# Cutting the run of small products in a fused attention and MLP kernel, and planning with other durations

## The chip, the cores and the metric

The kernel runs on one core of a Trainium2 chip. Time is device microseconds of one execution, and lower is better. Five engines work side by side: TensorE (PE in the profile, with its weight loads as PEld), VectorE (DVE), ScalarE (ACT), GpSimd (POOL) and SyncE (SP), which here issues most of the transfers. Each engine takes its instructions in the order in which the program gives them, and waits where an operand is not there yet.

## The reference

Two stages. The first is a linear attention with a state for each of 4 batches and 8 heads, over 768 time steps of 48 channels; the second is an MLP with a piecewise gate over the 3072 tokens that result.

```
for t in range(S):
    cur = einsum('bhd,bhe->bhde', u[None] * kt, vt)
    y[:, :, t] = einsum('bhd,bhde->bhe', rt, state + cur)
    state = wt[:, :, :, None] * state + einsum('bhd,bhe->bhde', kt, vt)
x = y as (3072, 384)
h = x @ w_in                     # 384 x 2048
g = where(h >= 1, h, where(h <= -1, 0, (h + 1)**2 / 4))
return g @ w_out                 # 2048 x 384
```

All inputs and the result are float32, and the kernel keeps that precision: in the MLP a float32 operand is split into a high and a low part, and three products of parts stand for one.

## The kernel before

**The attention** goes through twelve units (0 to 11), each 64 time steps of all batches, 256 tokens, as one chunk: within the chunk the products of r with k are formed as small matrices, across chunks a state of 48x48 per head is carried. A unit's work on TensorE is, in order: small 64x64 products of r with k ("among", L555; VectorE then picks the causal half of them into R, L561), transposes of k (L594, copied out by ScalarE, L603), and then the *run*: 16 products of r with the old state, crosswise between heads and groups ("cross", L667), 32 products of k times v for the new state ("umat", L624), and 48 more into the same two banks as the first (16 with the old state, 32 of R with v, "along", L667). Every float32 product of these is two instructions of the profile on TensorE and two weight loads, so the run is 192 products and 192 loads in the profile's counting. From k times v VectorE forms the new state (`stepped`, L642 and the fade behind it), which the next unit's cross needs; from the two banks the unit's y is brought into x (L739, L741).

In units 1 to 10 the three parts of the run are *glued* (`plan.glue`): nothing may stand between them on TensorE. Units 0 and 11 are not glued.

**The MLP** goes through six blocks of 512 tokens (two units each) with 16 steps over the hidden width. One step is nine wide products x by w_in into a bank (`product_in`, L1272), the gate (ScalarE L1084 and L1085, VectorE L1086, ScalarE's rounding L1088, VectorE's remainder L1089), and nine wide products of the gate by w_out into three accumulators (`product_out`, L1292). The first 5 steps of block 0 and the first 14 of block 1 work on the two halves of 256 tokens apart, so that the MLP starts with one unit done. The last block uses another scheme with fewer products (L984, finished by L1036). The weights arrive packed and are unpacked on the way, during the first half of the kernel (L441 to L454).

**What sets the order.** The program declares some thousand operations to a planner (class `Plan`), each with its engine, an assumed cost in us, a due time, what it reads and what it writes. `order` simulates the engines with these costs, taking on each engine the ready operation with the earliest key; a result may be used on another engine after `HOP`. `late` goes backward through such a plan to set new keys, and `best` keeps, of 40 randomly disturbed plans with a fixed seed, the one with the smallest planned end. [...] So a changed cost can move any operation, while the duration on the chip does not follow from it.

## Time and profile before

| what | value |
| --- | --- |
| time, median of three runs | 510.96 us (509.55 to 511.69) |
| the profiled execution | 510.8 us, of which the span is 509.2 us |
| granted clock of TensorE, mean | 0.994 |
| products and weight loads on TensorE | 5583 and 5583 |
| idle time of TensorE before products of L667, ended by "issue" | 9.1 us at six places |

Times stand in us. A row of the page's groups gives line, engine, operation, written from read tiles, partitions by elements, the count; then the busy time, the mean of one in ns, and the engine's idle time just before, with what ended most of it. "issue" means that the engine waited for nothing that the profile shows: no tile, no transfer, no semaphore. Rows of a timeline give the start, the duration, the instruction, and in brackets the idle time before it. The ends of products are modelled, so that starts are compared here where tenths of a us matter.

### The profile page before, as it was taken

Reading aid. Unit: us, or ns where it says so; the run is one execution under the profiler, and the core shown is the slowest. Engines: PE = TensorE matmul, PEld = TensorE weight load, DVE = VectorE, ACT = ScalarE, POOL = GpSimd, SP = SyncE. Lnnn points to the kernel's source line nnn. Section 1 sums busy time; section 2 is a strip of 40 time slices with the busy share of each in tenths; the row PEclk is TensorE's granted clock in tenths of the full one; section 3 lists DMA queues with packets and bytes.
Section 4 is the critical chain, followed back from the end, with each engine's and each line's share of the span. In section 5 each row is a group of like instructions: output and inputs, shape, how many; then the busy total and the mean of one; then the engine's idle time right before and its main releaser. Section 6 shows DMA issues by size and latency. Waiting matters only on the chain. (4 is left out here: it accounts for less than half of the span.)

```text
span 509.2 us, 13264 instructions
## 1 busy us (share of the span) xinstructions
PE 486.8 (96%) x5583; PEld 414.9 (81%) x5583; DVE 367.0 (72%) x631; ACT 305.6 (60%) x628; POOL 97.0 (19%) x80
## 2 busy tenths in 40 slices
PE   7778999999999999998999999999999999999994
PEld 5568988888889998877888887878878878889894
DVE  6899899988798888697963377854248544596653
ACT  4577979888866656565454556454365445575550
POOL 1654414411111111123010010200002402402000
PEclk9899999999999999999999999999999999999998
DMA  8977546245633350444320132400102000010002
GB/s 302 407 277 261 209 149 235 64 126 185 203 126 137 114 173 21 147 130 154 104 84 0 63 131 84 132 1 0 63 1 59 0 1 17 19 45 1 3 0 69
DMA packets 22052, 54.72 MB, mean 107 GB/s; under 512 B 3040, under 2 KB 9184, under 8 KB 21984
## 3 DMA queue, kind: packets, MB, share of 16 engines
q1 hardware_dynamic: 21840, 53.65, 30.6%
q8 instruction: 46, 0.75, 0.6%
q14 instruction: 22, 0.18, 0.1%
q10 hardware_dynamic: 144, 0.13, 0.1%
HBM read 47.09 MB, written 4.72 MB: 102 GB/s over the span
## 5 line engine op out<-in xcount | busy, mean ns | idle before, releaser
L1272 PE MATMUL h<-x,wt 128*128 128x512 f32 (+1 forms) x1035 | 219.4, 359 | 1.8 <-DVE x L739 1.5
L1272 PEld LDWEIGHTS h<-x,wt 128*128 128x128 f32 x1035 | 170.0, 188 | 32.5 <-DVE x L739 1.7
L1292 PE MATMUL acc<-gh,wt 128*128 128x512 f32 (+1 forms) x594 | 129.5, 353 | 0.0
L1292 PEld LDWEIGHTS acc<-gh,wt 128*128 128x128 f32 x594 | 97.6, 188 | 17.0
L1086 DVE SCALAR_TENSOR_TENSOR g<-g,h 128x512 f32<-128x512 f32 (+1 forms) x99 | 57.2, 578 | 70.2 <-ACT g L1085 69.9
L1084 ACT ACTIVATE g<-h 128x512 f32<-128x512 f32 (+1 forms) x99 | 50.9, 515 | 79.0 <-PE h L1272 68.0
L1292 PE MATMUL acc<-gl,wt 128*128 128x512 f32 (+1 forms) x297 | 72.1, 351 | 0.0
L1089 DVE TENSOR_TENSOR gl<-g,gh 128x512 fp32r<-128x512 f32 (+1 forms) x99 | 62.6, 642 | 7.8 <-ACT gh L1088 6.6
L1088 ACT CAST gh<-g 128x512 fp32r<-128x512 f32 (+1 forms) x99 | 52.5, 532 | 17.6 <-DVE g L1086 10.1
L1292 PEld LDWEIGHTS acc<-gl,wt 128*128 128x128 f32 x297 | 50.3, 188 | 8.4
L1085 ACT ACTIVATE g<-g 128x512 f32<-128x512 f32 (+1 forms) x99 | 54.5, 551 | 2.9
L581 POOL TENSOR_TENSOR r<-cst,d 128x512 f32<-128x512 f32 x18 | 19.7, 1113 | 168.5 <-PE bank L667 102.6
L449 POOL TENSOR_SCALAR wraw<-fl 128x768 uint16<-128x768 f32 x13 | 40.0, 3084 | 54.6 <-ACT wraw L447 54.6
L514 DVE TENSOR_TENSOR_SCAN p<-wq,seeds 128x520 f32<-128x520 f32 x24 | 32.3, 1346 | 3.2 <-DMA wq<-in_w 2.4
L573 POOL TENSOR_TENSOR nk<-nk 128x768 f32<-128x768 f32 x9 | 17.3, 1927 | 84.1 <-DMA nk<-in_nk 84.1
L509 DVE TENSOR_TENSOR_SCAN y<-wq,seeds 128x520 f32<-128x520 f32 x24 | 30.5, 1269 | 0.8
L945 DVE SCALAR_TENSOR_TENSOR rk<-rk,h 128x512 f32<-128x512 f32 x16 | 11.0, 687 | 18.3 <-ACT rk L944 18.0
L667 PE MATMUL bank<-r,vn 64*64 64x64 f32 (+1 forms) x768 | 15.4, 223 | 9.1 <-issue 9.1
L667 PEld LDWEIGHTS bank<-r,vn 64*64 64x64 f32 (+1 forms) x768 | 13.5, 135 | 9.9 <-issue 9.9
L942 ACT ACTIVATE rk<-h 128x512 f32<-128x512 f32 x16 | 9.6, 598 | 17.9 <-PE h L1272 17.7
L741 ACT CAST x<-bank 128x384 fp32r<-128x384 f32 x24 | 11.3, 485 | 12.3 <-PE bank L667 11.3
L561 DVE COPY_PREDICATED r<-below,bank 128x512 f32<-128x512 int32 x23 | 16.1, 734 | 3.3 <-PE bank L555 3.3
(198 smaller groups left out, 614.3 us busy)
## 6 DMA issues: line engine op xcount, KB each, us to landing
rk<-in_rk SPq DMA_DIRECT2D x24, 512.0 KB, 4.4
wraw<-in_wbits SPq DMA_DIRECT2D x16, 768.0 KB, 7.1
nk<-in_nk SPq DMA_DIRECT2D x9, 768.0 KB, 4.6
wq<-in_w SPq DMA_DIRECT2D x24, 260.5 KB, 3.0
vn<-in_v SPq DMA_DIRECT2D x12, 384.0 KB, 6.9
fl<-in_w SPq DMA_DIRECT2D x12, 260.0 KB, 2.9
out_y<-g SPq DMA_DIRECT2D x10, 256.0 KB, 2.6
x<-last SPq DMA_DIRECT2D x60, 32.0 KB, 2.5
```

The costliest lines, as they stand in the source:

```text
L449: op(on, 0.62 if f in SIGNS else 3.2, due, [("fl", k)], [("raw", f)], lambda: e.tensor_scalar(out=half(1), in0=s, scalar1=0.0, scalar2=327 ...
L509: V.tensor_tensor_scan(out=y_[:, ::-1], data0=w[:, SEG:0:-1], data1=sv[:, ::-1], initial=0.0, op0=ALU.mult, op1=ALU.add)
L514: V.tensor_tensor_scan(out=pv[:, q].rearrange("p n c -> p (n c)"), data0=w[:, 0:SEG], data1=sv, initial=0.0, op0=ALU.mult, op1=ALU.add,)
L581: op("POOL", 1.1, due, ["d", "cst"], [("R", h)], lambda h=h: G.tensor_tensor(out=r_[h], in0=twice.unsqueeze(1).unsqueeze(1).broadcast_to([ ...
L667: PE.matmul(out=bank[by[g]][HP * half : HP * half + M, lo : lo + C], start=first, stop=False, skip_group_check=True, **kw)
L1084: op("ACT", c, due, [("h", n)], [("g", gk)], lambda: nc.scalar.activation(gs, hs(), AF.Relu, scale=0.5, bias=0.5), uses=[hk])
L1085: op("ACT", c, due, (), [("g", gk)], lambda: nc.scalar.activation(gs, gs, AF.Square))
L1086: op("DVE", 0.13 + 0.53 * k, due, [("h", n)], [("g", gk)], lambda: nc.vector.scalar_tensor_tensor(out=gs, in0=gs, scalar=1.0, in1=hs(), op ...
L1088: op("ACT", c, due, [("g", gk)], [("gh", gk)], lambda: nc.scalar.copy(ghs, gs))
L1089: op("DVE", 0.15 + 0.5 * k, due, [("g", gk), ("gh", gk)], [("gl", gk)], lambda: nc.vector.tensor_tensor(out=gls, in0=gs, in1=ghs.bitcast(F ...
L1272: nc.tensor.matmul(hp, lhsT=wx[f][:, cs], rhs=xt[:, j, :], start=n == 0, stop=n == 8)
L1292: nc.tensor.matmul(o[j], lhsT=wx[f][:, cs], rhs=gt, start=first and i == 0, stop=stop and i == 2, skip_group_check=True)
```

## The change

Two things change. The run of the glued units is cut in two halves of 96 instructions each: cross and k times v stay glued, the update of the state is declared right behind them, and along becomes an operation of its own, which the planner may put later. And the planner gets other numbers: the time after which a result may be used depends on the engine that made it (`HOPS`), operations on VectorE and ScalarE overlap their successors a little (`OVERLAP`), and ten assumed costs differ. The operations themselves are the same, and so is their number, but for the zero products that the planner puts in. Lines of helpers move down by 11 (L667 is now L678, L624 is L635, L594 is L605), later ones by 9 (L1272 is now L1281, L1292 is L1301).

```diff
     HOP = 0.15
+    HOPS = {"PE": 0.2, "DVE": 0.05, "ACT": 0.06, "POOL": 0.08, "SP": 0.05}
+    OVERLAP = {"DVE": 0.07, "ACT": 0.09}
+
+    def after(self, m, n):
+
+        a, b = self.ops[m], self.ops[n]
+        if a["e"] == b["e"] and not a["size"]:
+            return 0.03 if a["e"] in self.OVERLAP else 0.0
+        return self.HOPS[a["e"]]
...
-            since[n] = max((back[m] + (0.0 if ops[m]["e"] == op["e"] and not op["size"] else self.HOP) for m in users[n]), default=0.0)
+            since[n] = max((back[m] + self.after(n, m) for m in users[n]), default=0.0)
...
-            back[n] = free[e] = t + ops[n]["cost"]
+            back[n] = t + ops[n]["cost"]
+            free[e] = back[n] - self.OVERLAP.get(e, 0.0)
             if ops[n]["port"]:
-                port = back[n]
+                port = free[e]
...
-            since[n] = max((end[m] + (0.0 if ops[m]["e"] == op["e"] and not ops[m]["size"] else self.HOP) for m in op["deps"]), default=0.0)
+            since[n] = max((end[m] + self.after(m, n) for m in op["deps"]), default=0.0)
...
-            free[e] = end[n] = t + op["cost"] * (2 if e == "PE" and t < RISES else 1)
+            end[n] = t + op["cost"] * (2 if e == "PE" and t < RISES else 1)
+            free[e] = end[n] - self.OVERLAP.get(e, 0.0)
             if op["port"]:
-                port = end[n]
+                port = free[e]
                 first.clear()
...
-                spare.append((end[n] + self.HOP, given[op["drop"]], n))
+                spare.append((end[n] + self.HOPS[e], given[op["drop"]], n))
...
-                op("PE", 0.4, due, [("k", slot[q]), "cst"], [("b", b)], lambda q=q, b=b: ktrans(q, b))
+                op("PE", 0.36, due, [("k", slot[q]), "cst"], [("b", b)], lambda q=q, b=b: ktrans(q, b))
...
         def multiplied():
-            return op("PE", 0.94 if glued else 1.27, due, [("kt", 0), ("kt", 1), vk], ukeys, umat, uses=lent.values())
+            return op("PE", 1.07 if glued else 1.27, due, [("kt", 0), ("kt", 1), vk], ukeys, umat, uses=lent.values())
 
         def stepped():
             for g in range(2):
-                op("DVE", 0.5, due, [ukeys[g], ("ptot", u, 0), ("ptot", u, 1)] + ([("s", old, g)] if u else []), [("s", new, g)],
+                op("DVE", 0.55, due, [ukeys[g], ("ptot", u, 0), ("ptot", u, 1)] + ([("s", old, g)] if u else []), [("s", new, g)],
                    lambda g=g: step(g), drop=lent[0] if glued and g else None)
                 if u:
-                    op("DVE", 0.47, due, [("ptot", u, 0), ("ptot", u, 1)], [("s", new, g)], lambda g=g: fade(g), port=True)
+                    op("DVE", 0.57, due, [("ptot", u, 0), ("ptot", u, 1)], [("s", new, g)], lambda g=g: fade(g), port=True)
...
         run = []
         if u:
-            run.append(op("PE", 0.6 if glued else 0.8, due, ss + [vk, ("r", slot[0]), ("r", slot[1])], [("b", by[0]), ("b", by[1])], cross, fresh=not alone,
+            run.append(op("PE", 0.64 if glued else 0.8, due, ss + [vk, ("r", slot[0]), ("r", slot[1])], [("b", by[0]), ("b", by[1])], cross, fresh=not alone,
                           grab=glued))
             if glued:
                 lent[0] = run[0]
             for g in range(2):
-                op("ACT", 0.35, due, [("b", by[g])], [("look", g)], lambda g=g: A.copy(look[0:1, g : g + 1], bank[by[g]][0:1, 0:1]))
+                op("ACT", 0.15, due, [("b", by[g])], [("look", g)], lambda g=g: A.copy(look[0:1, g : g + 1], bank[by[g]][0:1, 0:1]))
         if glued:
-            run.append(multiplied())
-        run.append(op("PE", (1.6 if glued else 1.74) if u else 1.27, due, ss + [("R", 0), ("R", 1), vk, ("r", slot[0]), ("r", slot[1])],
-                      [("b", by[0]), ("b", by[1])], along, fresh=False))
-        if glued:
-            plan.glue(*run)
-        elif goes_on:
+            plan.glue(*run, multiplied())
+            stepped()
+        op("PE", 1.74 if u else 1.27, due, ss + [("R", 0), ("R", 1), vk, ("r", slot[0]), ("r", slot[1])],
+           [("b", by[0]), ("b", by[1])], along, fresh=False)
+        if goes_on and not glued:
             multiplied()
-        if goes_on:
             stepped()
...
-        hk = op("PE", 2.15, due, [("wh", f), ("wl", f), *xs, *after], [("h", n)],
+        hk = op("PE", 2.1, due, [("wh", f), ("wl", f), *xs, *after], [("h", n)],
...
-            op("PE", 0.358 * len(todo), (n, -late * STEP - 0.1), reads, list(banks), lambda: accumulate(todo), fresh=fresh)
+            op("PE", 0.351 * len(todo), (n, -late * STEP - 0.1), reads, list(banks), lambda: accumulate(todo), fresh=fresh)
...
-        hk = op("PE", 2.15 * k, due, [("wh", f), ("wl", f), *xs, *after], [("h", n)],
+        hk = op("PE", 2.1 * k, due, [("wh", f), ("wl", f), *xs, *after], [("h", n)],
...
-        op("DVE", 0.15 + 0.5 * k, due, [("g", gk), ("gh", gk)], [("gl", gk)], lambda: nc.vector.tensor_tensor(
+        op("DVE", 0.17 + 0.54 * k, due, [("g", gk), ("gh", gk)], [("gl", gk)], lambda: nc.vector.tensor_tensor(
...
-            op("PE", 2.15 * k * len(terms) / 9, (n, -LAG * STEP * k), [("gh", gk), ("gl", gk), ("wh", f), ("wl", f)],
+            op("PE", 2.1 * k * len(terms) / 9, (n, -LAG * STEP * k), [("gh", gk), ("gl", gk), ("wh", f), ("wl", f)],
```

Three places show what the order of TensorE's instructions becomes. The first is unit 1, before: from the transposes of k (L594) to the first wide products after its run. `bank_`, `acc_` and `h_` tiles are banks of the accumulator memory, `x` the tokens, `wt` one step's weights, `gh` a gate.

```order
L594 MATMUL bank_118<-cst_67,rk_81 128x128 x4
L1272 MATMUL h_115<-x_95,wt_495 128x256 x9
L700 MATMUL bank_117<-zero_74 128x512
L667 MATMUL bank_118<-rk_81,st_93 48x64
L624 MATMUL bank_116<-vn_86,kt_92 64x48 x2
L667 MATMUL bank_117<-rk_81,st_93 48x64
L667 MATMUL bank_117<-r_90,vn_86 48x64
L1292 MATMUL acc_111<-gh_101,wt_393 128x256
```

Here it is after the change, with the new line numbers.

```order
L605 MATMUL bank_118<-cst_67,rk_81 128x128 x4
L414 MATMUL bank_116<-zero_74 128x108
L711 MATMUL bank_117<-zero_74 128x512
L678 MATMUL bank_118<-rk_81,st_93 48x64
L635 MATMUL bank_116<-vn_86,kt_92 64x48 x2
L1281 MATMUL h_114<-x_95,wt_533 128x256 x9
L678 MATMUL bank_117<-rk_81,st_93 48x64
L678 MATMUL bank_117<-r_90,vn_86 48x64
L1301 MATMUL acc_111<-gh_101,wt_386 128x256
```

The group of nine wide products that stood ahead of the run (h by x) stands now inside it, between k times v (L635) and along (L678), and zero products fill part of the place where it was.

The second place is unit 2 after the change, where the cut takes nine products of 512 columns (L1301); before, its run had no wide product in it, as in unit 1.

```order
L1281 MATMUL h_115<-x_95,wt_989 128x512 x9
L678 MATMUL bank_118<-rk_83,st_94 64x64
L635 MATMUL bank_116<-vn_85,kt_92 64x48 x2
L1301 MATMUL acc_111<-gh_103,wt_871 128x512
L678 MATMUL bank_117<-rk_83,st_94 64x64
L678 MATMUL bank_117<-r_90,vn_85 64x64
L1281 MATMUL h_114<-x_95,wt_1019 128x512 x9
```

Units 1, 2, 5, 7, 8 and 10 are cut by nine wide products, of 256 columns in 1 and 5 and of 512 in the others, and unit 3 by several groups. Units 4, 6 and 9 keep their run in one piece.

The third place is such an uncut unit, 4, after the change, with the groups that follow it. Each L1301 row stands for the group of nine that it begins.

```order
L678 MATMUL bank_117<-rk_81,st_94 64x64
L635 MATMUL bank_118<-vn_85,kt_92 64x48 x2
L678 MATMUL bank_117<-r_90,vn_85 64x64
L1281 MATMUL h_115<-x_96,wt_533 128x256 x9
L1301 MATMUL acc_111<-gh_103,wt_386 128x256
L1281 MATMUL h_114<-x_96,wt_625 128x256 x9
L1301 MATMUL acc_111<-gh_101,wt_401 128x256
L1281 MATMUL h_115<-x_96,wt_682 128x256 x9
L1301 MATMUL acc_111<-gh_102,wt_533 128x256
```

The run is as it was. Behind it the two kinds of groups alternate, so that between the end of the group that makes `wt_533`'s hidden values (L1281) and the group that uses their gate (L1301) stand 36 products of 256 columns; before, two or more groups of L1272 and L1292 in a row stood there.

## Prediction

> **What bounds the kernel now.** I read the page first: the span, the engines' shares, the slices.
>
> ```profile
> span 509.2 us, 13264 instructions
> PE 486.8 (96%) x5583; PEld 414.9 (81%) x5583; DVE 367.0 (72%) x631; ACT 305.6 (60%) x628; POOL 97.0 (19%) x80
> PE   7778999999999999998999999999999999999994
> PEclk9899999999999999999999999999999999999998
> q8 instruction: 46, 0.75, 0.6%
> L667 PE MATMUL bank<-r,vn 64*64 64x64 f32 (+1 forms) x768 | 15.4, 223 | 9.1 <-issue 9.1
> ```
>
> TensorE works in 96% of the span at an undisturbed clock, and only the first four slices (12.7 us each) and the last show it with time to spare. So the time is TensorE's work plus its idle 22.4 us (509.2 - 486.8), and a change of order can win only idle time or the cost of switching. The last row says where 9.1 us of that idle time lies: before products of L667, released by "issue", which means that no tile and no semaphore was late. The view of TensorE's waits, as a second step, shows how little else there is.
>
> ```profile
> PE bank L667 <- issue: 9.1, 6, 2.7
> PE h L409 <- POOL zero L388: 2.8, 1, 2.8
> PE h L1272 <- DVE x L739: 1.5, 1, 1.5
> ```
>
> Six waits for issue hold 9.1 us. The 2.8 us are the program's first wait, which the change leaves alone; the last row is unit 0's x, within the first 30 us. The timeline of TensorE names the six places (start, duration, instruction, idle time before it):
>
> ```profile
> 18.98 0.36 PE L667 MATMUL bank<-r,vn 64*48 64x64 f32 x4 [2.67 <-issue]
> 41.69 0.32 PE L667 MATMUL bank<-r,vn 64*48 64x64 f32 x7 [1.70 <-issue]
> 71.84 0.29 PE L667 MATMUL bank<-r,vn 64*64 64x64 f32 x5 [1.09 <-issue]
> 128.44 0.29 PE L667 MATMUL bank<-r,vn 64*64 64x64 f32 x5 [1.16 <-issue]
> 151.46 0.29 PE L667 MATMUL bank<-r,vn 64*64 64x64 f32 x5 [0.93 <-issue]
> 240.03 0.28 PE L667 MATMUL bank<-r,vn 64*64 64x64 f32 x4 [1.53 <-issue]
> ```
>
> What is late at such a place shows when the stretches between them are counted (windows: length, then busy us and records of PE, PEld, DVE, ACT, POOL, then clock, DMA share, GB/s):
>
> ```profile
> 18.97:41.68 22.71, 17.88 (x382) 13.88 (x383) 21.84 (x33) 17.39 (x34) 11.30 (x5) 0.93 0.75 287
> 41.68:71.83 30.15, 29.06 (x511) 27.44 (x511) 27.98 (x48) 25.88 (x56) 12.35 (x5) 1.00 0.54 194
> 71.83:128.43 56.60, 55.11 (x510) 46.26 (x510) 51.70 (x80) 48.34 (x94) 16.29 (x7) 1.00 0.49 167
> 128.43:151.45 23.02, 22.09 (x384) 21.51 (x384) 19.36 (x38) 17.21 (x47) 3.95 (x3) 1.00 0.51 166
> 151.45:240.02 88.57, 87.04 (x1274) 78.49 (x1273) 73.90 (x138) 52.90 (x128) 15.23 (x10) 1.00 0.38 123
> ```
>
> TensorE's records (products and weight loads) between stalls are 765, 1022, 1020, 768 and 2547: 3, 4, 4, 3 and 10 times 256, less 3, 2, 4, 0 and 13, which is what instructions that only wait would take, and those are not counted as records. The page's instruction queue brought 0.75 MB in 46 packets, 16 KB each, and 11,166 records over 46 are 243 per packet. So I read the stalls as TensorE waiting for its next 256 instructions. Wide products spend a block slowly (128 products of 0.117 or 0.233 us each); small ones spend it in under 2 us. Windows over the last 96 small records of a unit, stalled and clean, give the sizes:
>
> ```profile
> 38.92:42.14 3.22, 1.52 (x95) 1.37 (x96) 1.00 0.41 141
> 69.41:72.19 2.78, 1.69 (x95) 1.55 (x96) 1.00 0.44 99
> 125.93:128.72 2.79, 1.63 (x95) 1.49 (x96) 1.00 0.02 6
> 149.53:152.10 2.57, 1.64 (x96) 1.50 (x96) 1.00 0.62 160
> 237.16:240.38 3.22, 1.69 (x96) 1.56 (x96) 1.00 0.44 129
> 215.02:216.40 1.38, 1.38 (x96) 1.38 (x96) 1.00 0.05 12
> ```
>
> A clean run takes 1.38 us, the stalled ones 1.84, 1.40, 1.41, 1.19 and 1.84 more: **7.68 us** in the five units 1, 2, 4, 5 and 8. (Unit 0 holds the sixth stall, 2.67 us; its run was never glued and is not changed.) A pair of load and product takes 1.38/96 = 14.4 ns, so a block of 128 pairs is spent in 1.84 us, and the next is there 1.84 + 1.19 to 1.84 = 3.0 to 3.7 us after the boundary before. That is the bound to compare with. [...]
>
> **The change part by part.** *What is removed.* The run of 192 small pairs is cut between k times v and the products with R. The order of the changed kernel puts nine wide products into the cut in units 1, 2, 5, 7, 8 and 10 (in unit 3 several groups) and leaves units 4, 6 and 9 in one piece. A cut helps only if the block that would run out takes longer than 3.0 to 3.7 us. I counted the changed order's instructions in 256s, from the same start as before, and price each block that ends in a unit's small products at 14.4 ns a pair plus its nine wide products. Unit 1: 59 + 60 pairs around nine 256-wide ones, 1.71 + 1.05 + 0.2 for switching = 2.96 us, so a stall of 0 to 0.7. Unit 5 the same, 0 to 0.7. Units 2 and 8 have 512-wide ones: 1.71 + 2.10 + 0.2 = 4.0, none. Units 4, 6 and 9, uncut: boundaries fall into them, each block nearly all small, 1.85 to 2.04 us, so 1.0 to 1.8 each; of these only unit 4 stalled before. Together 3.2 to 6.7, and I take **5.0, near the middle, against 7.68: -2.7 us** (bounds -4.5 and -1.0).
>
> *What is added: switching.* A cut puts two more changes between wide and small products on TensorE. The trace has one such pair at unit 7:
>
> ```profile
> 212.78 0.87 PE L1292 MATMUL acc<-gl,wt 128*128 128x512 f32 x3
> 213.58 0.28 PE L667 MATMUL bank<-rk,st 64*64 64x64 f32 x3
> 216.54 4.46 PE L1272 MATMUL h<-x,wt 128*128 128x512 f32 x18
> 220.84 1.56 PE L1292 MATMUL acc<-gh,wt 128*128 128x512 f32 x6
> 222.24 0.86 PE L1292 MATMUL acc<-gl,wt 128*128 128x512 f32 x3
> ```
>
> Six wide products take 222.24 - 220.84 = 1.40 us, 0.233 each, so three should take 0.70; to the first small one it is 0.80: 0.10 in. The clean run above ends at 216.40, and the wide ones start at 216.54: 0.13 out beyond a pair's own time. Seven cuts at 0.23 are +1.6; two transposes that now stand together save a pair or so, 0.15. **+1.5 us** (bounds 0.7, if half of it hides under weight loads, and 2.0).
>
> *What moves: unit 1's start.* Before, nine 256-wide products stand between unit 1's last transposes and its run; now they stand inside the run.
>
> ```profile
> 35.42 0.66 PE L594 MATMUL bank<-cst,rk 128*128 128x128 f32 x4 [0.60 <-DVE r L561]
> 35.84 1.30 PE L1272 MATMUL h<-x,wt 128*128 128x256 f32 x9
> 36.98 0.61 PE L700 MATMUL bank<-zero 128*128 128x512 bf16 x2
> ```
>
> The group's starts lie 1.14 us apart (36.98 - 35.84). It covered the copies of the transposed keys on ScalarE, which do not come sooner; by the chain of r, transposes and copies the run starts only some 0.3 us earlier, with 1.14 us of products less behind it: **+0.8 us**, bounds +0.3 and +1.3 (all of it lost, or a quarter). What is late next is unit 1's x, which the 1.5 us wait for L739 shows to be short in this stretch already; the products that TensorE turns to then are the ones moved.
>
> *The planner's other numbers* reorder everything, but the durations on the chip do not change. Work on VectorE and ScalarE is the same in number; TensorE's wait rows after 42 us outside L667 sum to under 1 us, so nothing is to be had there (-0.6), and what a worse order costs is bounded by the second rival below (+2.5): **+0.3 us**. Zero fills grow by 206 columns, under 0.4 us, and stand where TensorE would wait anyhow. The end of the program keeps its order, last products, last sum on VectorE, output: 0.
>
> **Sum.** 510.8 (the profiled execution, whose span is 509.2) - 2.7 + 1.5 + 0.8 + 0.3 = 510.7. The median of the three runs is 510.96, so 0.16 over the profiled one: I forecast **510.8 us**, no difference that a measurement of this kernel can tell (about 0.5%, 2.5 us, to either side: 508.4 to 513.5). Its own range, adding the bounds: -4.5 + 0.7 + 0.3 - 0.6 = -4.1 and -1.0 + 2.0 + 1.3 + 2.5 = +4.8; they will not all fall on one side, so about half: 508.6 to 513.2.
>
> **The rivals.** *Faster: the stalls all but go.* If a block arrives at 3.0 us rather than 3.7, cut units never stall, and a boundary that drifts by some sixty instructions leaves units 6 and 9 clean as well. One stall of about 1.5 us stays in unit 4: -6.2, +1.5 for switches, 0 at the start: 506.3. For it: half of before's runs were clean by the same accident of position. Against it: three uncut units with a boundary inside each, by count.
>
> *Slower: TensorE waits for the gate.* The new costs let the planner put the second product of a feature group closer behind its first. Between the end of an L1272 group and its L1292 group the products in between took at least 5.3 us of TensorE's time before; now ten groups lie below that, most at 36 products of 256 columns, 36 x 0.117 = 4.2 us. What has to fit in between is this chain (two engines' timelines):
>
> ```profile
> 360.96 4.37 PE L1272 MATMUL h<-x,wt 128*128 128x512 f32 x18
> 363.91 0.60 ACT L1084 ACTIVATE g<-h 128x512 f32<-128x512 f32 x1 [1.68 <-DMA out_y<-g]
> 364.55 0.63 ACT L1085 ACTIVATE g<-g 128x512 f32<-128x512 f32 x1
> 365.21 0.69 DVE L1086 SCALAR_TENSOR_TENSOR g<-g,h 128x512 f32<-128x512 f32 x1 [3.83 <-ACT g L1085]
> 365.93 0.62 ACT L1088 CAST gh<-g 128x512 fp32r<-128x512 f32 x1 [0.75 <-DVE g L1086]
> 367.71 0.68 DVE L1089 TENSOR_TENSOR gl<-g,gh 128x512 fp32r<-128x512 f32 x1
> ```
>
> The first nine products end near 363.1 (360.96 + 9 x 0.233) and gl at 368.39: 5.3 us, of which the five operations are 3.2 and the rest queueing. The rival decides once queueing holds the chain above 4.2 us there. At 5.3 each place costs 1.1 us; since a wait at one place gives time to the next, I take three to four of the eight: +3.3 to +4.4, so 510.7 + 3.9 = 514.6. For it: VectorE is busy 51.70 of 56.60 us in the window from 71.83 to 128.43, so queues are long in that stage. Against it: half-wide operations are shorter than these, and the look-ahead of the planner counts the same chain.
>
> *The stalls only move.* The boundaries fall differently, and the three uncut units pay what five paid (units 1 and 5 with their 0.7 too): the stalls do not fall below 6.7. With switches and the start: 510.8 - 1.0 + 1.5 + 0.8 = 512.1. Or the six idle times have another cause than the next block, which a cut does not touch; then all 7.68 us stay and it is 510.8 + 1.5 + 0.8 = 513.1. For that: one kernel's six places are few. Against it: five stretches that all come out at multiples of 256. [...]
>
> **How the numbers follow.** Forecast 0.5, stalls go 0.22, the gate waits 0.15, stalls only move 0.13 (0.08 by position, 0.05 by another cause). Nine tenths of the first rival lie below 508.4 (0.20), and 0.04 of the forecast: faster 0.24. Three quarters of the gate's case lie above 513.5 (0.11), a quarter of the moved stalls (0.03) and 0.03 of the forecast: slower 0.17. The rest, 0.59, is no difference. For 8 in 10 I cut a tenth from either side: the lower end lies within the first rival's span, at 507.4, and the upper one within the gate's, at 514.0.
>
> **What would show it.** The idle time that "issue" released before the 64x64 products (the 9.1 us) should come to 5.9 to 9.4 with unit 0's 2.67, in units 4, 6 and 9 at 1.0 to 1.8 us each and in none of the units that were cut by 512-wide products. The L667 products (now L678) should keep their mean of 223 ns with some 14 more changes from wide to small. Unit 1 should start its run about 36.7 us. The forecast fails fast if waits of L1301 for "DVE gl" appear in TensorE's waits (slower), if issue falls below 4 us (faster), or if stalls stand elsewhere than at multiples of 256 instructions, which would take the ground from the count.

## The result: 1.35% slower

The changed kernel takes 517.41 us (median of four runs, 515.82 to 518.34) against 510.25 us; the ratio is 1.0135, with a 95% interval of 1.0096 to 1.0175. The forecast was 510.8 us and a range to 514.0, so the result lies outside it, on the slow side. The profiled execution took 518.34 us, 7.5 us more than that of before. One execution of all that follow, 522.82 us of the numbers alone, was in a slower state and is left out.

First its page, as the page of before was shown: the span, the engines, the slices, the small products, and ScalarE's rounding of the gate.

```profile
span 516.8 us, 13221 instructions
PE 494.3 (96%) x5587; PEld 417.0 (81%) x5587; DVE 364.9 (71%) x631; ACT 301.5 (58%) x628; POOL 100.0 (19%) x80
PE   7789999999998989999999999999999999999994
PEclk9799999999999999999999999999999999999998
L678 PE MATMUL bank<-r,vn 64*64 64x64 f32 (+1 forms) x768 | 15.0, 222 | 6.1 <-issue 6.1
L1097 ACT CAST gh<-g 128x512 fp32r<-128x512 f32 (+1 forms) x99 | 52.9, 535 | 32.3 <-DVE g L1095 29.5
```

The stalls for instructions went down, from 9.1 to 6.1 us (7.7 with one that stands under another name, below), as forecast, and TensorE's idle time is the same as before (516.8 - 494.3 = 22.5 us against 22.4). So the 7.5 us are in what the profile calls busy. That word hides them: a single product of 256 columns is drawn 0.36 us long (a row below), while the next can start after 0.117, so a product that comes some 0.2 us late, follows a product of another shape, or runs at half the clock leaves no idle time. The last row is a first hint; the same group of the page of before reads:

```profile
L1088 ACT CAST gh<-g 128x512 fp32r<-128x512 f32 (+1 forms) x99 | 52.5, 532 | 17.6 <-DVE g L1086 10.1
```

In the middle of the gate's chain ScalarE now stands idle for 32.3 us instead of 17.6. TensorE's idle time did not grow with it (22.5 us against 22.4); it says that the chain has less room around it. TensorE's waits in the changed kernel:

```profile
PE bank L678 <- issue: 6.1, 4, 2.8
...
PE h L1281 <- DVE st L653: 1.6, 1, 1.6
PE bank L605 <- DVE r L572: 1.1, 2, 0.9
PE h L1281 <- DVE g L1095: 1.0, 2, 0.8
```

The waits of L1281 for "DVE g" have grown from 0.3 us before to 1.0: the first products of a step wait until VectorE has read an earlier step's bank and so given it back. To see all of the loss I went through the starts of TensorE's products. Every product gets its undisturbed pace (0.233 us with 512 columns, 0.1165 with 256, 0.060, an estimate, for the attention's transposes and other 128-column products, of which the twelve below took 0.114 each; 0.0145 for a small one, nothing for zeros). In the kernel before the starts lie 0.234 and 0.117 us apart in the median with 512 and 256 columns. The paces sum to 452.7 us in every kernel here, since the work is the same. What a start comes later than that is put down to what stands at the place. One profiled execution of each kernel, in us:

| | before | changed | cut alone | numbers alone | cut, transfers 3.0 after 90 us |
| --- | --- | --- | --- | --- | --- |
| ahead of the first wide product, fetch apart | 15.2 | 17.7 | 16.5 | 19.4 | 15.6 |
| instruction fetch (unit 0 too) | 10.2 | 8.9 | 3.3 | 8.7 | 3.3 |
| changes between wide and small products | 7.9 | 10.0 | 11.1 | 7.7 | 11.2 |
| waits for other engines | 9.2 | 11.2 | 11.7 | 14.4 | 10.9 |
| zero products after the first wide one | 2.7 | 3.6 | 2.4 | 1.3 | 1.6 |
| pace | 1.7 | 2.4 | 2.2 | 3.1 | 1.6 |
| sum | 47.0 | 53.7 | 47.2 | 54.7 | 44.1 |
| time of this execution | 510.8 | 518.3 | 512.4 | 518.4 | 508.3 |

From before to changed the sum grows by 6.7 us, and 0.9 us more lie behind the start of the last product. The rows are rounded, and the line between waits and pace is a matter of choice. The three other columns are experiments, below.

One part of the larger start cannot be read off the order of instructions. TensorE's granted clock fell to one half behind unit 0's stall, for 3.4 us in this execution of the kernel before and for 6.8 us in that of the changed one. First the two stretches (window: length, TensorE's busy us and records, clock, DMA share, GB/s), then the same eight zero products in both, before and changed:

```profile
18.54:21.95 3.41, 2.97 (x33) 0.50 1.05 402
18.94:25.76 6.82, 6.30 (x37) 0.50 1.04 410
20.01 3.56 PE L403 MATMUL bank<-zero 128*128 128x512 f32 x8
20.48 5.01 PE L414 MATMUL bank<-zero 128*128 128x512 f32 x8
```

From their start to the next product they take 3.39 us before and 4.79 changed, and the twelve transposes behind them, from which unit 0's x is made, 1.37 and 1.61. So 1.6 us of the start belong to the clock. The columns of the cut alone and of the numbers alone have the same 6.8 us of half clock there, the last column has 3.4. It does not explain the result: the changed kernel's execution with a mean clock of 0.994, that of the profiled execution of before, took 515.82 us, still 5.0 us more. But it moves single executions: of 101 executions of the kernel before in the later comparisons, the 64 with a mean clock of 0.993 or more have a median of 510.07 us, the 21 with 0.991 or less 511.03.

### The profile page after: what moved, and what is told of

Its sections match the earlier page's. It is cut to its first block, busy times and chain, and to the rows that moved or that the text cites. A ratio compares the mean times of both kernels' runs of the same rounds, so it can differ in the third digit from the quotient of the medians.

```text
span 516.8 us, 13221 instructions
## 1 busy us (share of the span) xinstructions
PE 494.3 (96%) x5587; PEld 417.0 (81%) x5587; DVE 364.9 (71%) x631; ACT 301.5 (58%) x628; POOL 100.0 (19%) x80
## 5 line engine op out<-in xcount | busy, mean ns | idle before, releaser
L1281 PE MATMUL h<-x,wt 128*128 128x512 f32 (+1 forms) x1035 | 221.2, 361 | 3.0 <-DVE st L653 1.6
L1281 PEld LDWEIGHTS h<-x,wt 128*128 128x128 f32 x1035 | 169.4, 188 | 36.1 <-DVE g L1095 3.9
L1301 PE MATMUL acc<-gh,wt 128*128 128x512 f32 (+1 forms) x594 | 129.6, 353 | 0.0
L1301 PEld LDWEIGHTS acc<-gh,wt 128*128 128x128 f32 x594 | 97.5, 188 | 16.9
L1098 DVE TENSOR_TENSOR gl<-g,gh 128x512 fp32r<-128x512 f32 (+1 forms) x99 | 60.6, 615 | 22.5 <-ACT gh L1097 19.7
L1301 PE MATMUL acc<-gl,wt 128*128 128x512 f32 (+1 forms) x297 | 72.1, 351 | 0.0
L1097 ACT CAST gh<-g 128x512 fp32r<-128x512 f32 (+1 forms) x99 | 52.9, 535 | 32.3 <-DVE g L1095 29.5
L1301 PEld LDWEIGHTS acc<-gl,wt 128*128 128x128 f32 x297 | 50.3, 188 | 8.4
L460 POOL TENSOR_SCALAR wraw<-fl 128x768 uint16<-128x768 f32 x13 | 42.4, 3269 | 51.4 <-ACT wraw L458 44.3
L525 DVE TENSOR_TENSOR_SCAN p<-wq,seeds 128x520 f32<-128x520 f32 x24 | 30.0, 1251 | 3.1 <-DMA wq<-in_w 2.3
L678 PE MATMUL bank<-r,vn 64*64 64x64 f32 (+1 forms) x768 | 15.0, 222 | 6.1 <-issue 6.1
L750 ACT CAST x<-bank 128x384 fp32r<-128x384 f32 x24 | 11.2, 482 | 15.1 <-PE bank L678 14.3
L678 PEld LDWEIGHTS bank<-r,vn 64*64 64x64 f32 (+1 forms) x768 | 13.4, 135 | 6.7 <-issue 6.6
L748 DVE TENSOR_TENSOR x<-bank,x 128x384 fp32r<-128x384 f32 x22 | 12.1, 554 | 8.9 <-ACT last L750 5.4
```

The lines of the kernel that those rows point to most:

```text
L460: op(on, 0.62 if f in SIGNS else 3.2, due, [("fl", k)], [("raw", f)], lambda: e.tensor_scalar(out=half(1), in0=s, scalar1=0.0, scalar2=327 ...
L525: V.tensor_tensor_scan(out=pv[:, q].rearrange("p n c -> p (n c)"), data0=w[:, 0:SEG], data1=sv, initial=0.0, op0=ALU.mult, op1=ALU.add,)
L678: PE.matmul(out=bank[by[g]][HP * half : HP * half + M, lo : lo + C], start=first, stop=False, skip_group_check=True, **kw)
L1097: op("ACT", c, due, [("g", gk)], [("gh", gk)], lambda: nc.scalar.copy(ghs, gs))
L1098: op("DVE", 0.17 + 0.54 * k, due, [("g", gk), ("gh", gk)], [("gl", gk)], lambda: nc.vector.tensor_tensor(out=gls, in0=gs, in1=ghs.bitcast( ...
L1281: nc.tensor.matmul(hp, lhsT=wx[f][:, cs], rhs=xt[:, j, :], start=n == 0, stop=n == 8)
```

## Experiments: is it the cut or the planner's numbers?

The theory after the result (A): the loss is of the planner's new numbers; the cut wins its stalls and pays them back for switching. The rivals: the cut itself costs the 7 us (B), or the stalls are not blocks of instructions at all (C).

**The cut alone.** The kernel before with only this edit; costs, `HOP` and the rest stay.

```diff
-            run.append(multiplied())
-        run.append(op("PE", (1.6 if glued else 1.74) if u else 1.27, ... along, fresh=False))
-        if glued:
-            plan.glue(*run)
...
+            plan.glue(*run, multiplied())
+            stepped()
+        op("PE", 1.74 if u else 1.27, ... along, fresh=False)
```

> The kernel before with the cut alone: the planner keeps its old numbers, along keeps its cost of 1.74 as an operation of its own (it was planned with 1.6 inside the glued run). In its order all ten units are cut, and by count one block of 256 TensorE instructions is left that would run out in a cut run (unit 1, about 0.3 us) beside unit 0's stall. Theory A (the loss came from the planner's new numbers; stalls go where runs are cut, a cut costs 0.33 us of switching): the idle time ended by issue falls from 9.1 to 3.0 to 3.5 us, ten cuts cost 3.3 us, the start is as before: 507 us, 505.5 to 509. Rival B (the cut itself costs the 7 us, by the switches and by what it makes wait): 515 to 518 us. Rival C (the stalls are not the instruction blocks): issue stays at 9 us and the time is 511 to 514.

Measured: 509.51 us, ratio 0.9985 (0.9964 to 1.0005), no difference, and 0.5 us above what theory A allowed. Rival B is out. In TensorE's waits one for issue is left, unit 0's, and a new one stands beside it:

```profile
PE bank L667 <- issue: 3.1, 1, 3.1
PE h L409 <- POOL zero L388: 2.8, 1, 2.8
PE h L1272 <- DVE g L1086: 2.8, 1, 2.8
```

ScalarE's timeline shows where that comes from:

```profile
122.95 0.38 ACT L1084 ACTIVATE g<-h 128x256 f32<-128x256 f32 x1 [2.59 <-DMA out_y<-g]
```

The stalls of all ten units are gone (fetch 10.2 to 3.3 us in the table), 7 us won. Ten cuts pay 3.2 us for it, TensorE's waits grow by 2.5 and the start by 1.3, which is the longer half clock (its eight zero products take 4.79 us too). The 2.8 us wait is one place: ScalarE cannot begin a gate because block 0's output still leaves from the gate's tile. This execution took 512.40 us, and the ten runs 507.62 to 512.40, so the wait need not be that long in each. Its clock was half for 3.4 us more, from 124.1 us on, right at that wait.

**The numbers alone.** The changed kernel with the old gluing of the whole run.

```diff
-            plan.glue(*run, multiplied())
-            stepped()
...
+            run.append(multiplied())
+        run.append(op("PE", (1.6 if glued else 1.74) if u else 1.27, ... along, fresh=False))
+        if glued:
+            plan.glue(*run)
```

> The changed kernel with its planner's numbers but the run glued in one piece as before. By count nine blocks end inside small products of units 1 to 10, 10.4 us of stalls against 7.7 before, beside unit 0's. Theory A (the planner's numbers cost the time, by a later start, about 2.4 us, and by waits and zero products, about 3 us): no switches from cuts, more stalls, so 516 to 520 us with 11 to 14 us ended by issue. Rival B (the cut costs the time): 509 to 512 us.

Measured: 517.80 us (three executions, 514.71 to 518.39), ratio 1.0129 (1.0084 to 1.0173): the whole loss without any cut. (In this kernel L1281 stands at L1283.)

```profile
PE bank L678 <- issue: 7.6, 6, 2.8
PE h L1283 <- DVE g L1097: 3.5, 4, 1.7
...
PE bank L605 <- DVE r L572: 1.7, 2, 1.1
PE bank L566 <- DVE x L750: 1.2, 1, 1.2
```

The time fits theory A, the 11 to 14 us of issue do not: 7.6 were measured. The loss is in the start (+4.2 in the table, of which some 1.6 are the half clock) and in waits (+5.2), not in more stalls.

## Experiments: are the stalls blocks of 256 instructions?

**152 more instructions ahead of everything.** The changed kernel, its order untouched, with small zero products in place of a part of a zero fill.

```diff
-        for n in range(WARM):
+        for n in range(WARM + 40):
...
     def zeros(to, n, add):
+        n -= cut.pop() if cut else 0
```

With `cut = [1280]` only the first fill is shorter, by 1280 columns.

> The changed kernel with the order of every engine unchanged, but for 40 more of the small zero products with which TensorE begins and 1280 columns less of the first zero fill: 152 instructions more on TensorE ahead of unit 0, in time that it waits anyhow. Each boundary of 256 then falls 152 instructions earlier in the work. Theory A (stalls are blocks of 256 running out): by count unit 0 and unit 4 keep about 2.0 us in all, instead of 8.9, so 510.5 us, 509.5 to 512. Rival C (the stalls belong to the places, or to transfers at these times): no change, 516 to 519.

Measured: 514.59 us, ratio 1.0095 (1.0071 to 1.0120): 2.8 us less than the changed kernel, 2.0 by the two ratios, not 6.9. The waits:

```profile
PE h L1281 <- ACT x L750: 3.4, 1, 3.4
...
PE h L1281 <- DVE g L1095: 2.4, 4, 1.3
```

and the one stall that is left in TensorE's timeline, in unit 0:

```profile
17.40 0.73 PE L635 MATMUL acc<-vn,kt 64*64 64x48 f32 x34 [1.00 <-issue]
```

The stalls went as counted: 7.7 us of idle time became 1.0, with not one product moved in the order. Rival C is out. The count fits more than this run: taken over TensorE's products, weight loads and waits, all 59 idle times of its products named "issue" in the twenty profiled executions of this case stand 193 or 194 instructions over a multiple of 256.

But of 6.7 us won only 2 to 2.8 arrived. TensorE's idle times for other engines, without the program's first and the stall under another name, rose from 4.2 to 8.2 us: TensorE got to its products sooner and found x and the gate not ready. Unit 0 shows it. Its stall is 1.8 us shorter, yet the group of eight products that needs all of x starts at 28.91 us here and at 28.94 in the changed kernel, because VectorE and ScalarE bring x no sooner. And behind the wait for x the clock is half from 26.6 to 33.4 us, now under real products:

```profile
26.62:33.44 6.82, 5.11 (x76) 0.50 0.51 167
28.91 2.08 PE L1281 MATMUL h<-x,wt 128*128 128x256 f32 x8 [0.45 <-DVE x L748]
```

The same eight products are drawn 1.21 us long in the changed kernel.

**224 more instructions ahead of the kernel before.** The same edit with `WARM + 59` and `cut = [1536]`.

> The kernel before with its order unchanged, but for 59 more small zero products at the begin and 1536 columns less of the first zero fill: 224 instructions more ahead of unit 0. Theory A: by count the boundaries now fall inside eight of the ten glued runs, stalls of about 13.9 us in all against 10.2 before: 514 us, 512.5 to 515.5, with issue ending 12 to 14 us. Rival C: no change, 509.5 to 511.5.

Measured: 513.33 us, ratio 1.0074 (1.0047 to 1.0101). The time lies in the expected range, but not for the expected reason. Stalls as TensorE's timeline shows them:

```profile
11.04 0.53 PE L403 MATMUL bank<-zero 128*128 128x94 f32 x1 [0.88 <-issue]
21.50 0.43 PE L667 MATMUL bank<-r,vn 64*48 64x64 f32 x14 [1.25 <-issue]
45.59 0.32 PE L667 MATMUL bank<-r,vn 64*48 64x64 f32 x7 [1.04 <-issue]
75.73 0.28 PE L667 MATMUL bank<-r,vn 64*64 64x64 f32 x3 [1.04 <-issue]
...
243.69 0.33 PE L667 MATMUL bank<-r,vn 64*64 64x64 f32 x3 [1.19 <-issue]
```

Each, with two more at 132.21 and 155.42 us, stands at a counted boundary, and unit 0's moved as it should. But of eight blocks in the glued runs that would last under 2 us, three (from 176.3, 217.6 and 320.9 us on) ended after 1.9 us without a stall. In the numbers alone two of that kind passed too. So in these executions a boundary inside a run was needed for a stall, but not enough; what lets some blocks through stays open. The stalls sum to less than before (7.4 us of idle time against 9.1), and the 3.6 us came from the start: the first wide product begins at 28.16 us instead of 25.77, and waits for x follow. So the added products change more than the count. Unit 0's first products take 1.99 us in this kernel (first row) and 1.16 in the kernel before (second row), and VectorE waits for them (third row, this kernel; before, the same operation starts at 11.01 us with no idle time):

```profile
11.49 1.99 PE L555 MATMUL acc<-rk,nk 64*64 64x64 f32 x64
9.75 1.16 PE L555 MATMUL acc<-rk,nk 64*64 64x64 f32 x64
13.55 1.29 DVE L585 TENSOR_TENSOR rk<-rk,p 128x512 f32<-128x512 f32 x2 [2.81 <-PE acc L555]
```

A half clock of 6.8 us follows, from 30.1 us on. So the time of this run is no evidence for the count of stalls; that it lies in the range is luck.

## Experiments: which of the numbers?

**Hand-over times and overlap, old costs.** The changed kernel with its cost edits taken back (0.36 to 0.4, 1.07 to 0.94, and so on through the diff); along keeps 1.74.

> The changed kernel with its cut and its new hand-over times and overlap in the planner (HOPS, OVERLAP), but the old assumed costs. By count its stalls are 1.2 us fewer than the changed kernel's. Theory D (the short hand-over times leave the planner no room: it places each gate's chain so tightly that TensorE waits for it): 515 to 519 us, most of the loss. Theory E (the new costs do it, or the two only together): 508 to 512 us. Theory L (any new plan may fall that way, the draw decides): anything from 508 to 519.

Measured: 517.03 us, ratio 1.0115 (1.0074 to 1.0157).

**New costs, old hand-over time, no overlap.** The cut alone with those cost edits.

> The kernel with the cut alone and, in the planner, the ten new assumed costs but the old hand-over time of 0.15 us and no overlap. By count its stalls beside unit 0's are 2.7 us, against 0.3 with the cut alone. Theory D (the short hand-over times do it): 510 to 513 us, the cut alone plus its stalls. Theory E (the costs do it): 515 to 518 us.

Measured: 511.02 us, ratio 1.0004 (0.9984 to 1.0024). Theory D's forecasts came true in both: `HOPS` and `OVERLAP` carry the loss, the costs next to nothing. That lack of room is the reason is not shown by it.

**Is it the draw?** The planner keeps the best of 40 disturbed plans, so another seed is another order. The changed kernel with seed 2, and the cut alone with seed 3 (`SEED = 1` to 2 or 3).

> The changed kernel with another seed (2 for 1) for the planner's disturbances: same rules and costs, another order. By count 0.9 us more stalls than the changed kernel. If the loss is of the planner's numbers it comes back with another draw: 515 to 520 us, with TensorE waiting for gates and a first wide product after 27.5 us. If it was this draw's luck (theory L): 508 to 513 us.

> The cut alone with the planner's old numbers and another seed (3 for 1). By count only 0.8 us of stalls beside unit 0's, like the cut alone. If the old numbers make robust orders: 506 to 511 us. If the draw decides (theory L): it may be as far from 509.5 as the changed kernel, 514 or more.

Measured: 522.07 us (1.0216, 1.0167 to 1.0264) and 511.14 us (1.0008, 0.9984 to 1.0033), both just above their expected ranges. The draw moves a kernel by 1.6 us (cut alone) and 4.7 us (changed), and the changed kernel's own draw was the better of its two. But the loss came back with another draw, and the old numbers did not produce one. Theory L does not explain the result. It does limit what follows: each of the next kernels is one draw, so differences of 1 to 4 us between two of them are not yet their numbers'.

**Hand-over times without overlap, overlap without hand-over times.** From the 517.03 us kernel:

```diff
-    OVERLAP = {"DVE": 0.07, "ACT": 0.09}
+    OVERLAP = {"DVE": 0.0, "ACT": 0.0}
```

and, the other way round, `HOPS` at 0.15 everywhere and 0 on the same engine, with the overlap kept.

> The run of the cut with the short hand-over times (HOPS) and old costs, as in the run that gave 517.0 us, but without the planner's overlap of 0.07 and 0.09 us on VectorE and ScalarE. By count only 0.3 us of stalls beside unit 0's, 3.5 fewer than there. If the hand-over times leave too little room: 512 to 515 us, first wide product still 1.5 us or more later than before's 25.8 and more waits for gates than with the cut alone. If the overlap did it: 507 to 510.5 us.

> The reverse: the cut, old costs, the old hand-over time of 0.15 us everywhere, and the overlap of 0.07 and 0.09 us. By count 1.9 us of stalls beside unit 0's, 1.6 more than with the cut alone. If the overlap did it (the planner believes VectorE and ScalarE some 10% faster): 513 to 517 us. If the hand-over times did: 510 to 512 us.

Measured: 512.35 us (1.0041, 1.0023 to 1.0059) and 516.27 us (1.0129, 1.0109 to 1.0149). Over the cut alone the overlap costs 6.8 us, the hand-over times 2.8, together 7.5. The 2.8 are uncertain: the eight executions have mean clocks of 0.983 to 0.991, where the cut alone has 0.994 in most. The group of L1281 and ScalarE's rounding in the kernel with the overlap, from the page's groups:

```profile
L1281 PE MATMUL h<-x,wt 128*128 128x512 f32 (+1 forms) x1035 | 220.4, 361 | 4.3 <-DVE g L1095 3.0 <-DVE st L653 1.1 <-DVE wt L465 0.3
L1097 ACT CAST gh<-g 128x512 fp32r<-128x512 f32 (+1 forms) x99 | 53.0, 536 | 38.0 <-DVE g L1095 34.7 <-PE acc L1301 2.3 <-PE h L1281 0.6
```

Five waits for a bank, and 38.0 us of ScalarE idle inside the gate's chain; its first wide product starts at 31.17 us, behind waits of 2.17 us for ScalarE and 1.11 us for VectorE.

**More room than before.** The cut alone with `HOP = 0.30` for 0.15.

> The cut alone with twice the hand-over time in the planner, 0.30 us for 0.15, all else as before. By count 1.9 us of stalls beside unit 0's. If room for the gate's chain is what decides, more room costs nothing or wins: 506 to 510.5 us with fewer waits for gates than with the cut alone. If it is rather that any number that differs from the old one spoils the order: 513 us or more.

Measured: 511.29 us, ratio 1.0018 (1.0003 to 1.0034), a little slower, between the two forecasts. So it is no straight line: less room than the old numbers cost 3 to 7 us in these draws, more won nothing.

**The overlap taken out of the changed kernel.**

> The changed kernel, whole, but with the planner's overlap set to 0 on VectorE and ScalarE: the cut, the short hand-over times and the new costs stay. By count its stalls are 1.0 us less than the changed kernel's, counted the same way with unit 0's. If the overlap is the main part of the loss: 511 to 513.5 us. If it is the sum of many numbers: 515 to 518.

Measured: 514.04 us, ratio 1.0062 (1.0040 to 1.0085), just above the expected range. In the whole change the overlap is 3.4 us of 7.2, the largest single part, and not all.

**The overlap on one engine.** Old hand-over time, old costs, the cut, and the overlap on ScalarE or on VectorE alone.

> The cut, old costs, old hand-over time of 0.15 us, and the overlap on ScalarE alone (0.09 us). By count 1.8 us of stalls beside unit 0's. ScalarE heads each gate and its transposed keys. If ScalarE's overlap is the harmful one: 514 to 517 us, and its partner 509 to 512. If either does its part: both 511 to 514.

> The same with the overlap on VectorE alone (0.07 us). By count 0.7 us of stalls beside unit 0's. VectorE is 96% busy from 24 to 100 us in the kernel before, so that planned room there is dearest: if that decides, 514 to 517 us, and its partner 509 to 512.

Measured: 510.78 us (1.0001, 0.9977 to 1.0026) and 513.33 us (1.0062, 1.0040 to 1.0083). Neither of the two forecasts fits: VectorE's costs 3.8 us over the cut alone, less than "the harmful one" was to cost, and ScalarE's 1.3, which its stalls (fetch 5.4 us against 3.3) more than cover and which the draw could give alone. What single kernels cannot show, all of them together support: the seven orders planned with VectorE's overlap take 513.3 to 522.1 us, the eleven planned without it 508.2 to 514.0.

Yet the overlap agrees with the trace. VectorE's timeline in the kernel before:

```profile
99.48 0.68 DVE L1086 SCALAR_TENSOR_TENSOR g<-g,h 128x512 f32<-128x512 f32 x1
100.08 0.55 DVE L739 TENSOR_TENSOR x<-bank,x 128x384 fp32r<-128x384 f32 x1
100.55 0.68 DVE L1089 TENSOR_TENSOR gl<-g,gh 128x512 fp32r<-128x512 f32 x1
```

An operation of 0.68 us is followed after 0.60, one of 0.55 after 0.47: 0.08 us of overlap each. Over all operations that follow one another without a wait the mean is 0.08 us on VectorE (421 of them) and 0.10 on ScalarE (293). The planner that reckons with it made the worse orders.

**Late transfers as the reason.** One thing that the durations could not repair is the transfers' time. The changed kernel, and the cut alone, with

```diff
-                end[n] = bus + 2.0
+                end[n] = bus + 3.5
```

> The changed kernel, whole, with the planner reckoning 3.5 us instead of 2.0 from a transfer's last byte to its use, the change that won 0.6 us with the cut alone. By count 1.7 us fewer stalls than the changed kernel. If accurate durations hurt because transfers come later than planned, and the old ones covered that: 508 to 512 us. If they hurt for other reasons: 514.5 to 518.

> The cut alone, with the planner reckoning 3.5 us instead of 2.0 from a transfer's last byte to its use. The cut alone lost 2.8 us at one place, near 122 us: ScalarE waited for the output of block 0 to leave the gate's tile (2.59 us, ended by the transfer), and TensorE for that gate. By count only 0.3 us of stalls beside unit 0's. If the wait goes: 506 to 508.5 us, below both kernels. If the order is otherwise worse for it: 509 to 512.

Measured: 514.19 us (1.0056, 1.0028 to 1.0084) and 508.87 us (0.9974, 0.9960 to 0.9988). In the changed kernel 3.2 us come back, between the two forecasts. Its profiled execution has some 3 us less of stalls (5.6 against 8.9, by the starts of the products; 1.7 were counted), as much as was won, and its first wide product starts still later (32.04 us). So late transfers are not shown to be any part of it. That VectorE, which is busy in 72.8 of the 76 us from 24 to 100 us in the kernel before, needs planned room is the reading that is left; no run shows it by itself, and I leave the cause of the worse order at: VectorE's overlap first, the short hand-over times likely second, the mechanism between them and the waits only argued.

**A version that beats both.** The second kernel above does, by 0.26%. It lost time at its start (first wide product at 29.34 us). It lies 0.4 us above the range that was expected if the wait near 122 us goes, and the wait did go. With the longer transfer time for later transfers only, two more kernels:

```diff
-                end[n] = bus + 2.0
+                end[n] = bus + (2.0 if t < 90.0 else 3.0)
```

> The cut alone, with 3.5 us for 2.0 from a transfer's last byte to its use, but only for transfers that are planned after 20 us. With 3.5 us throughout the kernel took 508.9 us, and lost 2.4 us ahead of its first wide product, which came later; by count stalls are as with the cut alone. If the start comes back (first wide product near 26 us) and the wait at 122 us stays away: 506 to 508 us, below both kernels. If the order falls otherwise: 508.5 to 511.

> The same with 3.0 us, and only for transfers planned after 90 us, so that the first 90 us may be planned as with the cut alone, which was 1.6 us ahead of the kernel before at 112 us and lost it at 122 us. If that one wait was the loss: 505.5 to 508 us. If the wait only moves: 509 to 511.

Measured: 509.71 us (0.9992, 0.9979 to 1.0006) with 20 us and 3.5, and **508.16 us (0.9957, 0.9940 to 0.9974)** with 90 us and 3.0: faster than before by 0.4%, and than the changed kernel by 9.3 us. The first fell into its second range, the second 0.2 us above its first one. The waits of the latter:

```profile
PE bank L667 <- issue: 2.7, 1, 2.7
PE h L1272 <- DVE x L739: 1.1, 1, 1.1
PE h L1272 <- DVE g L1086: 0.9, 2, 0.5
```

The long wait near 122 us is 0.5 now. Since draws of this planner differ by 1.6 us and more, how much of the 1.3 us over the cut alone is that wait, and how much luck, the runs don't tell apart.

## Why the prediction was wrong, step by step

**What bounds the kernel** was right: TensorE, and stalls for blocks of 256 instructions in runs of small products. One reading was not: the clock is no "undisturbed" one, it is half for 3.4 us behind unit 0's stall (the 8 in the row PEclk), and the sum had no term for it. The timeline of the changed kernel shows the stalls again:

```profile
19.46 0.45 PE L678 MATMUL bank<-r,vn 64*48 64x64 f32 x5 [2.79 <-issue]
164.82 0.39 PE L1281 MATMUL h<-x,wt 128*128 128x256 f32 x2 [1.63 <-DVE st L653]
188.58 0.40 PE L678 MATMUL bank<-r,vn 64*64 64x64 f32 x13 [1.57 <-issue]
243.69 0.41 PE L678 MATMUL bank<-r,vn 64*64 64x64 f32 x13 [1.22 <-issue]
341.47 0.45 PE L678 MATMUL bank<-r,vn 64*64 64x64 f32 x14 [0.58 <-issue]
```

The second row names VectorE, but it stands at the end of unit 4's uncut run, on a counted boundary, and it is not there in the kernel with 152 instructions more. It is a stall under another name: the page's 6.1 us of issue are 7.7 in truth.

**The stalls, -2.7 forecast.** By the start of the products -1.3 (10.2 to 8.9), inside the bounds of -4.5 to -1.0. Units 4, 6 and 9 stalled as named (1.8, 1.4 and 0.8), unit 1 with 0.2, and no unit cut by 512-wide products did. Unit 5 paid 1.8 where 0 to 0.7 was forecast: its block lasted 3.1 us, but the next came only 4.9 us after the boundary before, later than any of the 3.0 to 3.7 on which the bound rested.

**Switching, +1.5 forecast, +2.0 measured.** I priced a cut at 0.23 us. It costs 0.33, as unit 2's cut shows in the changed kernel:

```profile
78.31 1.66 PE L1301 MATMUL acc<-gh,wt 128*128 128x512 f32 x6
79.81 0.86 PE L1301 MATMUL acc<-gl,wt 128*128 128x512 f32 x3
80.60 0.34 PE L678 MATMUL bank<-rk,st 64*64 64x64 f32 x8
```

The first six products take 1.50 us, not 1.40: the second wide product after small ones comes 0.10 us late. The prediction's own fence held this (18 products in 220.84 - 216.54 = 4.30 us, for 4.19 at 0.233), and I read only its ends.

**Unit 1's start, +0.8 forecast.** The loss is there, but ahead of the place. The wide work begins 2.5 us later:

```profile
27.74 0.75 PE L414 MATMUL bank<-zero 128*128 128x256 f32 x4
28.31 0.36 PE L1281 MATMUL h<-x,wt 128*128 128x256 f32 x1
28.94 1.21 PE L1281 MATMUL h<-x,wt 128*128 128x256 f32 x8 [0.26 <-DVE x L748]
```

The first wide product stood at 25.77 us before. Of these 2.5 us, 0.5 stand already at the end of unit 0's run, 1.6 are the half clock under the zero products and the transposes behind them, and 0.4 two more zero products. The group that needs all of x starts 1.3 us later (28.94 against 27.61). I had looked at this for the one group of products that changed place, neither at the whole order up to the first wide product nor at the clock. Zero products cost 0.9 us later on, not nothing.

**The planner's numbers, +0.3 forecast, bounds -0.6 to +2.5.** This is the step that failed. The numbers alone, without the cut, cost 8.1 us (517.80 against 509.68 in the same comparison; 6.6 by the ratio), far above the upper bound. I bounded them by the gate's chain between a step's first and second products, and in the changed kernel TensorE does not wait for that (no wait of L1301 is among its waits). It waits at L1281 for the bank that the same chain gives back, for x, and in the start; none of these had a bound. Why the planner's truer numbers lead to such orders stays open.

**The end, 0 forecast, +0.9.** The last work lies differently. SyncE's queue in the changed kernel:

```profile
508.77 1.70 SPq L1060 DMA_DIRECT2D out_y<-g  x2
510.57 0.55 SPq L1060 DMA_DIRECT2D out_y<-rk  x1
511.21 0.40 SPq L1060 DMA_DIRECT2D out_y<-ob  x1
511.71 0.41 SPq L1060 DMA_DIRECT2D out_y<-g  x1
```

Before, two transfers of g go ahead of the last three too, but they begin 1.7 us ahead of the start of the last product (500.68 and 502.40 us), here 0.3 us (508.77 and 509.09). So the last issue begins 2.6 us after that start; before it was 1.6 us (503.96).

**The rivals.** "TensorE waits for the gate", 514.6 us at 0.15, was the right side and the right chain; its place and size were not. "The stalls only move" was true of unit 5 alone. "The stalls all but go" comes true with the cut alone, and even there the time did not fall, which the forecast of 506.3 for it had left out: time that TensorE won at a stall was partly lost again at the next wait.

## What to carry to other kernels

Here a run of small products spent 256 instructions in 1.84 us, while at most stalls the next ones came 2.9 to 3.7 us after the boundary before. In a kernel that stalls so, count them in such blocks along the order, and put something long (512-wide products here) into each block that would end too soon. Even so, only what the next wait does not take back arrives: 2 to 2.8 of 6.7 us with the 152 instructions. A change with two parts is to be taken apart before it is judged: here one part was worth nothing by itself and the other cost everything. Durations that agree with the trace, as the overlap did, need not make a better plan; that the longer ones served as a safety margin is a guess that fits these runs. And where a difference of 1 or 2 us counts, the granted clock of each profiled execution is to be read first, and one draw of a randomized planner is no proof.

## What the runs showed of the hardware

- TensorE's idle times named "issue" stand at multiples of 256 of its products, weight loads and waits (plus 193 or 194), all 59 in twenty profiled executions. In most, the next block comes 2.9 to 3.7 us after the boundary before; six behind unit 0 took 3.9 to 5.9 us, and unit 0's 5.5 to 6.0 us where its order was not shifted by added products. Of 41 blocks behind unit 0 that were spent in 2.5 us or less, 7 passed with no stall at all, in 1.9 to 2.3 us.
- From small to wide products TensorE loses 0.13 us ahead of the first and 0.10 ahead of the second wide product, from wide to small 0.09: the same in the kernels before and changed, at all 30 changes to wide and 28 to small that no wait preceded.
- TensorE's granted clock falls to one half for 3.4 or 6.8 us at a time, up to the last products. In each of the 17 profiled executions whose unit 0 stalled for 2.3 us or more it did so, beginning within that stall or up to 1.2 us behind it; in the three with a stall of 1.0 to 1.6 us there it did not.
- VectorE's and ScalarE's records overlap by 0.08 and 0.10 us in the kernel before, on average, where one operation follows another without a wait (421 and 293 times).
